# One quarter of the output weights ahead of two v tiles in the load queue, and the scaling of those tiles later on VectorE

## The chip, the cores and the metric

The kernel runs on one core of a Trainium2 chip. The metric is the time of one execution on the device, in microseconds; lower is better. Each comparison runs both kernels in turn on the same chip. A run counts as fast unless it lies more than 1.5% above the fastest of its kernel; ratios use fast runs alone.

## The reference, cut to what matters

Attention with a learned decay, then a feed-forward network on its result:

```python
scores = q @ k.T / sqrt(64)                       # 8 batches x 8 heads, 576 x 576, causal
bias   = -(cum[i] - cum[j])                       # cum = cumsum(max(s, 0))
attn   = softmax(scores + min(bias, 0))
x      = (attn @ v) -> 4608 tokens x 512
out    = gelu(x @ w_in) @ w_out                   # w_in 512 x 2048, w_out 2048 x 512
```

The kernel uses that the row part of the bias cancels in the softmax: it multiplies row j of v, and a column of ones that gives the denominator, by exp(cum[j]). So every v tile is *scaled* by VectorE before it is used.

## The kernel before

The 4608 tokens are worked in 9 chunks of 512. In chunk c TensorE does layer 1 (`w_in`), then layer 2 (`w_out`), and attention of batch c + 1 is woven into layer 2, item by item, so that TensorE never has to stand. Within chunk 0 the loads have not finished yet. The order of the transfers is that of GpSimd's program:

```python
def load_w(which, i):            # a quarter of w_in or w_out: fp32 in HBM, bf16 in SBUF
    ...
        dst = w_out_r[:, i * 4 : (i + 1) * 4, :]          # 4 of the 16 row tiles
    nc.gpsimd.dma_start(out=dst, in_=src)

# start-up (cut)
load_qks(1)
load_w(1, 0)
load_w(1, 1)
load_v(1, nc.gpsimd, (0, 1))     # v tiles 0 and 1 of batch 1
load_w(1, 2)                     # "quarter 2": row tiles 8 to 11 of w_out
load_w(1, 3)                     # "quarter 3": row tiles 12 to 15
load_v(1, nc.gpsimd, (2, 3, 4))
...
# layer 2 of chunk 0 (cut): side[i] is what stands behind the i-th group of matmuls
side[0] = [(sc, b, 0, 0), (scale_v, b, 0), (scale_v, b, 1), (mk, b, 0, 0)]
side[3] = [(sc, b, 1, 0), (to_xT, 0, 4, True), (mk, b, 1, 0)]
side[5] = [(sc, b, 0, 1), (av, b, 0, 0), (av, b, 0, 1)]
side[6] = [(av, b, 1, 0, True), (av, b, 1, 1, True), (scale_v, b, 2), (mk, b, 0, 1)]
...
groups(c, (0, 1), side[:8])      # group i: row tiles 2i and 2i+1, for two blocks of 128 tokens
```

`sc` is a score unit: matmuls on TensorE, then two exponentials on ScalarE. `mk` applies the causal mask (VectorE), `scale_v` scales a v tile (VectorE), `av` is an attention product (TensorE, then two short steps of VectorE), `to_xT` transposes a finished tile (TensorE, then a VectorE copy). A group is four matmuls. Groups 4 and 5 need quarter 2; groups 6 and 7 need quarter 3.

Of the kernel before, what the change touches and what calls it, by code (L numbers as in the profile page):

```python
# [19 lines left out]
def kernel(  # L20
# [89 lines left out]
    def load_qks(b):  # L110
        load_qk(b, 0)
        load_qk(b, 1)

    def raw_v(b):
        raws[b, "v"] = work.tile([128, ST, H, D], fp32, tag="rawv", bufs=2, name="raw_v")
        return raws[b, "v"]

    def load_v(b, eng, sts=range(ST)):
        t = raws[b, "v"] if (b, "v") in raws else raw_v(b)
        for st in sts:  # L120
            n_st = 128 if st < ST - 1 else SL
            eng.dma_start(  # L122
                out=t[:n_st, st, :, :],
                in_=bass.AP(
                    tensor=v.tensor,
                    offset=v.offset + b * H * S * D + st * 128 * D,
                    ap=[[D, n_st], [S * D, H], [1, D]],
                ),
            )
# [11 lines left out]
    def load_w(which, i):  # L141
        if which == 0:
            src = moe_w_in.rearrange("(ko p) f -> p ko f", p=128)[:, :, i * 512 : (i + 1) * 512]
            dst = w_in_r[:, :, i * 512 : (i + 1) * 512]
        else:
            src = moe_w_out.rearrange("(fo p) m -> p fo m", p=128)[:, i * 4 : (i + 1) * 4, :]
            dst = w_out_r[:, i * 4 : (i + 1) * 4, :]
        nc.gpsimd.dma_start(out=dst, in_=src)
# [64 lines left out]
    def square_v(b, st):  # L213
        n_st = 128 if st < ST - 1 else SL
        sq = work.tile([128, H * D], bf16, tag="sq", bufs=2, name="sq")
        nc.scalar.activation(  # L216
            sq[:n_st], raws[b, "v"][:n_st, st].rearrange("p h d -> p (h d)"), func=AF.Square,
            accum_out=sumv[:n_st, b, st : st + 1],
        )
# [11 lines left out]
    def den_col(b):  # L231
        nc.vector.tensor_copy(vv[b % 2][:, :, :, D], wb[:, :, b * H : (b + 1) * H])
# [228 lines left out]
    def l1_item(c, f2, n0=0, n1=NB):  # L461
        if f2 == 0 and n0 == 0:
            gT_of[c] = work.tile([128, FT, NB], bf16, tag="gT", bufs=1, name="gT")
        if n1 - n0 < NB and f2 % 4 < 2:
            h_ps = yps.tile([128, 2, NB // 2], fp32, tag="mlp", bufs=2, name="h2_ps")
        else:
            h_ps = ps.tile([128, 2, NB], fp32, tag="sc", bufs=2, name="h_ps")
        h_ps = h_ps[:, :, : n1 - n0]
        for i in range(2):
            ft = f2 * 2 + i  # L470
            for ko in range(KO):
                nc.tensor.matmul(  # L472
                    h_ps[:, i, :], lhsT=w_in_r[:, ko, ft * 128 : (ft + 1) * 128],
                    rhs=xT[:, ko, c * NB + n0 : c * NB + n1],
                    start=(ko == 0), stop=(ko == KO - 1),
                )
        nc.scalar.activation(  # L477
            gT_of[c][:, f2 * 2 : f2 * 2 + 2, n0:n1], h_ps, func=AF.Gelu
        )
# [24 lines left out]
    def exp_set():  # L504
        nc.scalar.preload_act_table_set("natural_log_exp_and_others")  # L505
# [29 lines left out]
    load_qks(1)  # L535
    load_w(1, 0)
    load_w(1, 1)
    load_v(1, nc.gpsimd, (0, 1))
    load_w(1, 2)
    load_w(1, 3)  # L540
    load_v(1, nc.gpsimd, (2, 3, 4))
    tr_qk(0, 0, 0)
# [30 lines left out]
    sc, mk, av = sc_item, mk_item, av_item  # L573
# [5 lines left out]
    for c in range(NCH):  # L579
        b = c + 1  # L580
        if c > 0 and b + 1 < B:
            load_qks(b + 1)
            load_v(b + 1, nc.gpsimd)
        if c == 0:

            late = [
                [], [], [], [], [(av, 0, 0, 2), (av, 0, 1, 2)],
                [(av, 0, 0, 3), (av, 0, 1, 3)], [(to_xT, 0, 2, True), (to_xT, 0, 3, True)],
                [], [(scale_v, 0, 4), (av, 0, 0, 4)], [(av, 0, 1, 4)],
            ] + [[]] * 6  # L590
            for half in range(2):
                for f2 in range(FT // 2):
                    l1_item(0, f2, half * 256, half * 256 + 256)
                    for f, *a in late[8 * half + f2]:
                        f(*a)
                    if f2 % 2 and 3 <= 8 * half + f2 <= 11:
                        square_v(0, 4 * half + f2 // 2 - 1)
        else:
            for f2 in range(FT // 2):
                l1_item(c, f2)  # L600
                for g, it in late_of.get(c, [])[f2 : f2 + 1]:
                    av(c, g, it)
                if b < B and f2 < HG:
                    tr_qk(b, 0, f2)
                    tr_qk(b, 1, f2)
                if b < B and f2 == 2:
                    den_col(b)
                    for st in range(2):
                        scale_v(b, st)
                if b < B and f2 == 3:  # L610
                    for st in range(2, ST):
                        scale_v(b, st)
                if b < B and 4 <= f2 < 4 + HG:
                    absmax(b, f2 - 4)
                if c == 2 and f2 == 7:
                    cert_decay()
                if f2 < ST and c < B:
                    square_v(c, f2)
        if b < B:
            if c == 0:  # L620
                for g in range(HG):
                    for i in range(2):
                        tr_qk(b, i, g)
                den_col(b)
            exp_set()
            if c == 0:
                load_qks(2)
                load_v(2, nc.gpsimd)
                side = [[] for _ in range(16)]
                side[0] = [(sc, b, 0, 0), (scale_v, b, 0), (scale_v, b, 1), (mk, b, 0, 0)]  # L630
                side[3] = [(sc, b, 1, 0), (to_xT, 0, 4, True), (mk, b, 1, 0)]
                side[5] = [(sc, b, 0, 1), (av, b, 0, 0), (av, b, 0, 1)]
                side[6] = [(av, b, 1, 0, True), (av, b, 1, 1, True), (scale_v, b, 2), (mk, b, 0, 1)]
                side[7] = [(to_xT, b, 0, True), (sc, b, 1, 1)]
                side[8] = [(to_xT, b, 1, True), (scale_v, b, 3), (av, b, 0, 2), (gelu_set,), (mk, b, 1, 1)]
                side[9] = [(av, b, 0, 3)]
                side[11] = [(av, b, 1, 2, True), (scale_v, b, 4), (square_qk, 0, 0, 0), (square_qk, 0, 0, 1)]
                side[12] = [(av, b, 1, 3, True), (square_qk, 0, 1, 0), (square_qk, 0, 1, 1)]
                side[13] = [(to_xT, b, 2, True)]
                side[14] = [(to_xT, b, 3, True)]  # L640
                groups(c, (0, 1), side[:8])
                for sub in (2, 3):
                    groups(c, (sub,), side[4 * sub : 4 * sub + 4])
            else:

                side = [[] for _ in range(16)]
                sc_at = (1, 4, 6, 8) if b < 4 else (1, 4, 7, 10)
                for at, (g, u) in zip(sc_at, [(0, 0), (1, 0), (0, 1), (1, 1)]):
                    side[at].append((sc, b, g, u))
                side[sc_at[3]].append((gelu_set,))  # L650
                mk_at = (4, 6, 8, 10) if b < 4 else (4, 7, 10, 13)
                for at, (g, u) in zip(mk_at, [(0, 0), (1, 0), (0, 1), (1, 1)]):
                    side[at].append((mk, b, g, u))
                for at, (g, it) in zip((5, 6, 8, 9), [(0, 0), (0, 1), (1, 0), (1, 1)]):
                    side[at].append((av, b, g, it))
                if b < 4:
                    side[10].append((av, b, 0, 2))
                    side[11].append((av, b, 1, 2))

                    side[15].extend([(av, b, 0, 3), (av, b, 1, 3)])  # L660
                if c == 1:
                    side[0].append((absmax, c, 0))
                    side[12].extend([(square_qk, c, 1, 0), (square_qk, c, 1, 1)])
                    side[3].append((cert_exp,))
                for sub in range(4):
                    groups(c, (sub,), side[4 * sub : 4 * sub + 4])
        else:
            for sub in range(4):
                l2_item(c, (sub,), store=(c, sub) < LAST)
                if c == B - 1:  # L670
                    (cert_1, cert_2, cert_3, cert_4)[sub]()
                elif sub == 0:

                    rv = nc.values_load(bad[0:1, 0:1], min_val=0, max_val=1)
# [169 lines left out]
```

## Time and profile before

| | before |
|---|---|
| median of 3 runs | 313.47 us (312.7 to 313.74) |
| span of the profile | 311.6 us |
| TensorE busy | 304.0 us, 98% |
| VectorE, ScalarE busy | 196.5, 193.3 us |
| TensorE's waits after the first 8 us | one, 0.52 us, for a quarter of w_out |

"Busy" is the time in which an engine has an instruction under way, "span" the time from its first to its last. How to read the table: TensorE is the bound nearly everywhere, so an instruction of another engine, or a transfer, costs time only where TensorE has to stand for it. The lines that carry this are in the prediction.

How to read the lines of the profile: start in us, length in us, engine (PE is TensorE, DVE VectorE, ACT ScalarE, POOL GpSimd), line of the kernel, operation, what it writes `<-` what it reads, shapes, number of instructions (x8), and in brackets how long the engine stood idle before it and what ended that. Idle times under 0.15 us are not noted, and they count from the modelled end of the instruction before, so a delay can be somewhat larger than its bracket. x7 or x3 where the program has 8 or 4 matmuls means that a record is missing from the trace. The tiles: `o_ps` is layer 2's output and `av` an attention product, both in PSUM, the memory that TensorE writes its results to; `sc_ps` are scores, `P` their exponentials, `xt_ps` transposes.

### The profile page before, as it was taken

What the parts mean: (1) busy time and instruction counts of PE and PEld (TensorE: products, weight loads), DVE (VectorE), ACT (ScalarE), POOL (GpSimd) and SP (SyncE); (2) the same over time, 40 slices, a digit from 0 to 9 for tenths busy, and PEclk for the clock granted to TensorE, in tenths of its full rate; (3) what the DMA queues carried; (4) which work ended last, traced back from release to release, by engine and by line L of the source; (5) the groups of instructions that cost most, each with busy time, mean ns of one, the idle gap of its engine ahead of it and who ended that gap; (6) DMA issues with size and microseconds to landing.
All of it is one profiled execution on the core that took longest, in us unless ns stands there. A gap on an engine that the chain in (4) does not pass through costs nothing. (4 is left out here: it accounts for less than half of the span.)

```text
span 311.6 us, 6102 instructions
## 1 busy us (share of the span) xinstructions
PE 304.0 (98%) x2511; PEld 155.1 (50%) x2511; DVE 196.5 (63%) x397; ACT 193.3 (62%) x262; POOL 53.2 (17%) x72
## 2 busy tenths in 40 slices
PE   6999999999999999999999999999999999999994
PEld 2579655444554455445454545444544555444441
DVE  6976667697769775966498549955895632250010
ACT  2787868878858772974687548765776667105500
POOL 8373340142002400060007000500000000000000
PEclk9999999999999999999999999999999999999999
DMA  7999999769640974089208941633101311010012
GB/s 150 213 231 209 225 216 284 153 139 202 159 99 17 213 171 119 8 177 212 86 18 175 219 95 30 144 69 103 50 19 42 103 53 25 34 68 36 0 69 76
DMA packets 33027, 36.73 MB, mean 118 GB/s; under 512 B 17760, under 2 KB 22112, under 8 KB 32992
## 3 DMA queue, kind: packets, MB, share of 16 engines
q0 software_dynamic: 11472, 22.81, 37.3%
q1 hardware_dynamic: 20336, 12.93, 14.9%
q10 hardware_dynamic: 1184, 0.52, 0.6%
q8 instruction: 21, 0.34, 0.4%
q14 instruction: 14, 0.11, 0.1%
HBM read 36.85 MB, written 9.44 MB: 149 GB/s over the span
## 5 line engine op out<-in xcount | busy, mean ns | idle before, releaser
L488 PE MATMUL o_ps<-w_out_r,gT 128*128 128x512 bf16 x576 | 135.6, 379 | 0.5 <-DMA w_out_r<-in_moe_w_out_dram 0.5
L472 PE MATMUL h_ps<-xT,w_in_r 128*128 128x512 bf16 (+1 forms) x640 | 131.6, 358 | 0.0
L477 ACT ACTIVATE gT<-h_ps 128x1024 bf16<-128x1024 f32 (+1 forms) x80 | 75.1, 938 | 65.7 <-PE h_ps L472 64.7
L472 PEld LDWEIGHTS <-w_in_r 128*128 128x128 bf16 x640 | 60.0, 98 | 54.3 <-issue 0.3
L488 PEld LDWEIGHTS <-gT 128*128 128x128 bf16 x576 | 52.0, 98 | 57.4 <-issue 3.3
L364 ACT ACTIVATE P<-sc_ps 128x1024 bf16<-128x1024 f32 x56 | 54.3, 1021 | 25.8 <-PE sc_ps L349 25.8
L500 DVE COPY o_sb<-o_ps 128x512 f32<-128x512 f32 x30 | 20.7, 691 | 55.7 <-PE o_ps L488 55.7
L122 POOL DMA_DIRECT2D raw_v<-in_v_dram x39 | 33.1, 858 | 126.3 <-ACT sq L216 115.2
L188 DVE STREAM_TRANSPOSE qkT<-raw_qk 128x576 f32<-128x576 f32 x32 | 37.2, 1238 | 0.0
L450 DVE TENSOR_TENSOR x<-av,rc 128x256 bf16<-128x256 f32 (+1 forms) x80 | 33.8, 423 | 3.0
L449 DVE RECIPROCAL rc<-av 128x4 f32<-128x4 f32 (+1 forms) x80 | 14.1, 176 | 34.2 <-PE av L440 34.1
L440 PEld LDWEIGHTS <-P 128*128 128x128 bf16 x576 | 26.5, 98 | 15.8 <-DVE P L372 1.6
L208 DVE TENSOR_REDUCE amx<-raw_qk 128x2 f32<-128x2304 bf16 x13 | 32.7, 2535 | 0.0
L440 PE MATMUL av<-vv,P 128*128 128x65 bf16 x576 | 30.2, 193 | 0.1
L224 DVE TENSOR_TENSOR vv<-raw_v,wb 128x512 bf16<-128x512 f32 (+1 forms) x39 | 25.3, 691 | 3.6 <-DMA raw_v<-in_v_dram 3.6
L216 ACT ACTIVATE sq<-raw_v 128x512 bf16<-128x512 f32 (+1 forms) x40 | 24.8, 621 | 0.0
L372 DVE TENSOR_TENSOR P<-P,tri_bf 128x1024 bf16<-128x1024 bf16 (+1 forms) x33 | 22.7, 692 | 3.3 <-ACT P L364 3.2
L349 PE MATMUL sc_ps<-qkT 32*128 32x256 bf16 (+2 forms) x560 | 18.0, 250 | 0.0
L349 PEld LDWEIGHTS <-qkT 32*128 32x128 bf16 x560 | 11.7, 92 | 12.2 <-issue 8.5
L505 ACT ACT_TABLE_LOAD x8 | 10.3, 1283 | 1.3 <-PEq L828 1.2
L424 PE MATMUL f_ps<-zero 128*128 128x512 bf16 x30 | 9.8, 451 | 1.2 <-DVE zero L151 1.2
L508 ACT ACT_TABLE_LOAD x8 | 10.3, 1283 | 0.1
(80 smaller groups left out, 92.6 us busy)
## 6 DMA issues: line engine op xcount, KB each, us to landing
out_dram<-o_sb SPq DMA_DIRECT2D x34, 256.0 KB, 2.2
raw_v<-in_v_dram POOLq DMA_DIRECT2D x31, 256.0 KB, 5.8
raw_qk<-in_q_dram POOLq DMA_DIRECT2D x7, 576.0 KB, 7.8
raw_qk<-in_k_dram POOLq DMA_DIRECT2D x7, 576.0 KB, 10.7
w_in_r<-in_moe_w_in_dram POOLq DMA_DIRECT2D x4, 512.0 KB, 10.5
w_out_r<-in_moe_w_out_dram POOLq DMA_DIRECT2D x4, 512.0 KB, 15.9
raw_v<-in_v_dram POOLq DMA_DIRECT2D x8, 128.0 KB, 6.0
raw_qk<-in_q_dram POOLq DMA_DIRECT2D x2, 288.0 KB, 6.2
```

Of the source, the lines that this page charges most:

```text
L122: eng.dma_start(out=t[:n_st, st, :, :], in_=bass.AP(tensor=v.tensor, offset=v.offset + b * H * S * D + st * 128 * D, ap=[[D, n_st], [S * D ...
L188: nc.vector.transpose(qkT[b % 2][:, i, g, :S, :].rearrange("p s e -> p (s e)").bitcast(fp32) .rearrange("p (l j) -> p j l", j=LT), raws[b, ...
L208: nc.vector.tensor_reduce(amx[:, b * HG + g], raws[b, "qk"][:, :, g, :], axis=AX, op=ALU.max, apply_absolute_value=True,)
L216: nc.scalar.activation(sq[:n_st], raws[b, "v"][:n_st, st].rearrange("p h d -> p (h d)"), func=AF.Square, accum_out=sumv[:n_st, b, st : st ...
L224: eng.tensor_tensor(vv[b % 2][:n_st, st, :, 0:D], raws[b, "v"][:n_st, st, :, :], w.unsqueeze(2).to_broadcast([n_st, H, D]), op=MULT,)
L349: nc.tensor.matmul(s_ps[h // 2][:, h % 2, off : off + n], lhsT=qk[r, 1, g, jt * 128 : jt * 128 + 128, e], rhs=qk[r, 0, g, i0 : i0 + n, e], ...
L364: nc.scalar.activation(P[:, 2 * h2 : 2 * h2 + 2, o : o + 512], s_ps[h2], func=AF.Exp, scale=scale)
L440: nc.tensor.matmul(o_ps[:, h, :], lhsT=P[:, h, off : off + 128], rhs=vv[b % 2][:, jt, 4 * g + h, :], start=(i == 0), stop=(i == len(BLK[it ...
L450: nc.vector.tensor_tensor(x_of[b, it][:n, g * 256 : g * 256 + 256].rearrange("p (h d) -> p h d", d=D), o_ps[:n, :, 0:D], rc[:n].unsqueeze( ...
L472: nc.tensor.matmul(h_ps[:, i, :], lhsT=w_in_r[:, ko, ft * 128 : (ft + 1) * 128], rhs=xT[:, ko, c * NB + n0 : c * NB + n1], start=(ko == 0) ...
L477: nc.scalar.activation(gT_of[c][:, f2 * 2 : f2 * 2 + 2, n0:n1], h_ps, func=AF.Gelu)
L488: nc.tensor.matmul(y_of[c, sub], lhsT=gT[:, ft, sub * 128 : (sub + 1) * 128], rhs=w_out_r[:, ft, :], start=(ft == 0), stop=(ft == FT - 1),)
```

## The change

The intent: bring quarter 2 of w_out earlier, since TensorE stands for it, and let VectorE wait for the two v tiles only after it has done the mask and the copy that need no v.

```diff
     load_w(1, 1)
+    load_w(1, 2)
     load_v(1, nc.gpsimd, (0, 1))
-    load_w(1, 2)
     load_w(1, 3)
@@
-                side[0] = [(sc, b, 0, 0), (scale_v, b, 0), (scale_v, b, 1), (mk, b, 0, 0)]
-                side[3] = [(sc, b, 1, 0), (to_xT, 0, 4, True), (mk, b, 1, 0)]
+                side[0] = [(sc, b, 0, 0), (mk, b, 0, 0)]
+                side[3] = [
+                    (sc, b, 1, 0), (to_xT, 0, 4, True), (scale_v, b, 0), (scale_v, b, 1), (mk, b, 1, 0)
+                ]
```

## The prediction

> **What bounds the kernel now.** I read the busy shares first, then all that TensorE ever waited for, then the order of time around the one wait that the change can touch.
>
> ```profile
> PE 304.0 (98%) x2511; PEld 155.1 (50%) x2511; DVE 196.5 (63%) x397; ACT 193.3 (62%) x262; POOL 53.2 (17%) x72
> ```
>
> TensorE is busy 304.0 of the 311.6 us span, and the granted clock is full in every slice of the page. VectorE and ScalarE stand at 63% and 62%. So an instruction of VectorE, ScalarE or the transfer queue costs time only where TensorE is made to stand still. The list of TensorE's waits says where it did (engine, line, cause: us, times, longest):
>
> ```profile
> PE t_ps L247 <- ACT cum L241: 1.6, 1, 1.6
> PE f_ps L424 <- DVE zero L151: 1.2, 1, 1.2
> PE o_ps L488 <- DMA w_out_r<-in_moe_w_out_dram: 0.5, 1, 0.5
> ```
>
> These are all. The first two lie in the first 8 us, before the stage the change touches. The third is the whole target: 0.52 us, once, on the third quarter of w_out. TensorE's order of time shows it (start, length, operation, then the idle time before it):
>
> ```profile
> 39.34 0.63 PE L349 MATMUL sc_ps<-qkT 32*128 32x256 bf16 x16
> 39.91 0.29 PE L415 MATMUL xt_ps<-ident_bf,x 64*128 64x64 bf16 x4
> 40.71 1.89 PE L488 MATMUL o_ps<-w_out_r,gT 128*128 128x512 bf16 x8 [0.52 <-DMA w_out_r<-in_moe_w_out_dram]
> 42.53 0.64 PE L349 MATMUL sc_ps<-qkT 32*128 32x256 bf16 x24
> ```
>
> This is layer 2 of chunk 0. After the second score unit (39.34) and four small transposes (39.91, modelled end 40.19), the eight matmuls on w_out rows of the third quarter can't start before 40.71. VectorE in the same stretch:
>
> ```profile
> 37.52 0.70 DVE L224 TENSOR_TENSOR vv<-raw_v,wb 128x512 bf16<-128x512 f32 x1 [2.23 <-DMA raw_v<-in_v_dram]
> 38.51 0.69 DVE L224 TENSOR_TENSOR vv<-raw_v,wb 128x512 bf16<-128x512 f32 x1 [0.29 <-DMA raw_v<-in_v_dram]
> 39.20 0.69 DVE L372 TENSOR_TENSOR P<-P,tri_bf 128x1024 bf16<-128x1024 bf16 x1
> 40.23 0.29 DVE L418 COPY xT<-xt_ps 128x256 bf16<-128x256 bf16 x1 [0.34 <-PE xt_ps L415]
> 41.98 0.69 DVE L372 TENSOR_TENSOR P<-P,tri_bf 128x1024 bf16<-128x1024 bf16 x1 [1.46 <-ACT P L364]
> 43.44 0.18 DVE L449 RECIPROCAL rc<-av 128x4 f32<-128x4 f32 x1 [0.76 <-PE av L440]
> ...
> 45.78 0.68 DVE L224 TENSOR_TENSOR vv<-raw_v,wb 128x512 bf16<-128x512 f32 x1
> ```
>
> It scales v tiles 0 and 1 of batch 1 as they land (37.52, 38.51), masks the first P tile (39.20), copies a transposed tile to xT (40.23), masks the second P tile (41.98), and at 43.44 takes up the first attention output. ScalarE's exponentials, which feed the masks:
>
> ```profile
> 37.23 1.94 ACT L364 ACTIVATE P<-sc_ps 128x1024 bf16<-128x1024 f32 x2
> 40.01 1.94 ACT L364 ACTIVATE P<-sc_ps 128x1024 bf16<-128x1024 f32 x2 [0.84 <-PE sc_ps L349]
> ```
>
> GpSimd's issues of the transfers that the change reorders (w_out quarter 1; v tiles 0 and 1; w_out quarters 2 and 3):
>
> ```profile
> 20.14 0.75 POOL L148 DMA_DIRECT2D w_out_r<-in_moe_w_out_dram  x1 [0.99 <-DMA w_in_r<-in_moe_w_in_dram]
> 21.71 1.86 POOL L122 DMA_DIRECT2D raw_v<-in_v_dram  x2 [0.82 <-DMA raw_v<-in_v_dram]
> 25.33 1.51 POOL L148 DMA_DIRECT2D w_out_r<-in_moe_w_out_dram  x2 [1.76 <-DMA w_in_r<-in_moe_w_in_dram]
> ```
>
> Looking at one issue at a time, the time to landing counts from the start of the issue: w_out quarter 1 16.3 us, v tiles 15.8 each, quarter 2 15.3, quarter 3 17.4. So the landings are: quarter 1 at 20.14 + 16.3 = 36.44; v0 at 21.71 + 15.8 = 37.5; v1, issued about 22.65, at 38.45; quarter 2 at 25.33 + 15.3 = 40.63; quarter 3 at about 26.1 + 17.4 = 43.5. The consumers agree: VectorE starts at 37.52 and 38.51, TensorE at 40.71. A v tile takes about 1.0 us of this queue and quarter 2 takes 40.63 - 38.45 = 2.18 us.
>
> **What the Trainium skill says.** "DMA: Bandwidth & Descriptors", section "Two DMAs through the same engine are not ordered": descriptors of one queue on one DMA engine start in order, but are pipelined, so only the completion semaphore tells that data has landed. The trace agrees as far as it shows: issued in the order quarter 1, v0, v1, quarter 2, they land in that order 1.06, 0.95 and 2.18 us apart. This is what lets me treat the swap as an exchange of places in a line.
> "TensorE: Matmul & The Clock Gate", section "Wait — 56ns, not 53.3ns?": a warm matmul of 512 columns starts 215.7 ns after the one before. The trace's layer 2 run of 16 matmuls from 84.08 to 87.54 gives 3.46/16 = 0.216 us, so the cadence is already the floor, and the 379 ns mean in the table of groups is overlapped length. Same page, section "What's actually happening": the clock falls after an idle window of about 3.4 us. The wait of 0.52 us is far shorter and the clock record stays full, so removing it brings no second gain through the clock.
> The same page, section "Architectural detail: the array is 16× 32×32, not 1× 128×128", says that VectorE's queue is strictly first in, first out. So a scaling that waits for v holds up every later instruction of VectorE. The trace fits: at 38.51 VectorE waits for v1, while P's exponentials end at 37.23 + 1.94 = 39.17, and nothing of later order runs before. That is why the change has to move the scalings too.
>
> **The change part by part.** It adds and removes no instruction; the compiled order of VectorE and GpSimd differs at these places, and TensorE, ScalarE and the store queue keep theirs.
>
> 1. Transfers. Quarter 2 goes ahead of v0 and v1. It lands at 36.44 + 2.18 = 38.62 instead of 40.63. v0 lands at 38.62 + 1.06 = 39.7 (2.2 later), v1 at 40.65 (2.2 later). After the three the line is as before, so quarter 3 (43.5), v2 (27.98 + 17.2 = 45.2) and the rest should land as before.
>
> 2. TensorE. It reaches the third quarter at 40.19 at the latest; the data has then been there for 1.5 us. The 0.52 us go. Its weights were loaded at 40.12 and the transposes are tiny, so it may be up to 0.1 us more.
>
> 3. VectorE. Now mask (0,0) follows the column copy, and runs at about 39.2 (end of the exponentials, 39.17) to 39.85, as before. The xT copy stays at 40.23 to 40.5. Scaling v0: landed 39.7, so 40.5 to 41.2. Scaling v1: landed 40.65, so 41.2 to 41.8. Two scalings of 0.69 us thus go into the hole of 1.46 us before 41.98 that waits for ScalarE's exponentials (40.01 + 1.94 = 41.95). Mask (1,0) still starts at 41.98. So VectorE gains and loses nothing: the waits at 37.5 and 38.5 vanish and the 1.46 us hole is filled.
>
> 4. Who needs those results next. The first attention product stood at 43.10 and comes at about 42.58; it needs v0 scaled (41.2) and the second product v1 scaled (41.8). Slack: 1.4 and 1.0 us. The products on the second P tile come at 43.8 and need mask (1,0), done at 42.65.
>
> Sum: TensorE gets 0.52 us, less at most 0.1 us of new small waits (below), plus at most 0.1. I take 0.5 us. There is no other TensorE wait in the remaining 270 us that could swallow it, and the chain at the end is layer 2, two half copies and a store, so it should reach the end whole. 313.47 - 0.5 = 312.97. The other two runs of before (312.7, 313.74) give a mean of 313.30, so the median may stand a little high; I say 312.9.
>
> **Rivals.** (a) *The score tiles become the wait.* Score unit (0,1) moves from 42.53 to 42.01. It writes two PSUM tiles, and the second comes free only when ScalarE's second exponential ends at 41.95. The margin shrinks from 0.58 to 0.06 us, about the time of a handover (mask (1,0) started 0.03 after). This can take back 0 to 0.1 us, which is in the sum. It would give 313.0 to 313.1.
> (b) *v arrives late.* If small v packets suffer from neighbours and v1 lands after 42.1, then VectorE's queue holds mask (1,0) and the second attention product. v1 would have to be 1.4 us later than I work out for the product to feel it. Against it: 0.95 to 1.06 us each for v0 and v1 in the same stretch. Result if true: gain falls to 0 to 0.3 us, 313.2 to 313.5.
> (c) *The next transfer becomes the wait.* Quarter 3 lands at 43.5; TensorE wants it at 44.94 now and at 44.4 after: 0.9 us of slack. v2 lands at 45.2; VectorE's scaling stood at 45.78 with no wait and would now come at about 45.26: hardly a wait, and only on VectorE. Each issue of GpSimd also waits for the landing of the transfer eight places before it (33.83, 36.44, 37.5 landing; issues at 34.10, 36.75, 37.78), so the k load of batch 2, which waited for v0, now waits for quarter 2 and is issued about 1.1 us later. Some 15 us of transfers stand in line then, and k landed at 37.78 + 15.4 = 53.2 while its first transpose ran at 58.10. It can't matter.
> (d) *Nothing at all.* The wait is hidden anyway, or the gain drowns: runs of before spread over 1.04 us, twice the gain. The first half I hold for unlikely, as TensorE is the bound on both sides of the wait; the second is likely for a single pair of runs.
>
> **Range and chances.** The step is 0.3 to 0.65 us with confidence; the spread of a median of a few runs is about 0.3 us and so is the uncertainty of the 313.47. Together 312.3 to 313.6. Two per cent is 6.3 us, twelve times all that is at stake, and no wait in the stretch could grow so far: v landing several us late would be needed. I give 0.985 to within 2%.
>
> **What would show it.** In the changed kernel: TensorE's list of waits has lost the line on w_out, or keeps under 0.1 us; the eight matmuls after the small transposes start near 40.15; the score unit (0,1) near 42.0, and ScalarE's next pair of exponentials at about 42.7 instead of 43.21; VectorE shows mask, copy, scaling, scaling, mask with the second mask still at 41.98 to 42.0; quarter 2 lands near 38.6, v0 near 39.7, v1 near 40.7; the span is 311.1. I am wrong if quarter 2 still lands after 40.2, if VectorE waits for v past 42, or if TensorE stands as long at another place, such as the scores at 42 or quarter 3.

## The result, and the profile after

| | before | after |
|---|---|---|
| median of 5 runs | 313.47 us (312.7 to 314.35) | 312.9 us (312.3 to 313.32) |
| ratio of fast runs | | 0.998 (95%: 0.9956 to 1.0004) |
| span of the profile | 311.6 us | 311.5 us |

The ratio is the mean time of the one kernel's fast runs over that of the other's in the same rounds, so not quite the ratio of the medians. The median fell on the predicted 312.9. But the interval of the ratio contains 1, and the profiled span did not fall by 0.5 us as it should have; it fell by 0.1. (That profile was taken of the slowest of the five runs, 313.32 us.) So the profiles have to say what happened.

TensorE's waits in the profile after, all of them (engine, line, cause: us, times, longest), are two, both in the first 9 us:

```profile
PE t_ps L247 <- ACT cum L241: 2.1, 1, 2.1
PE f_ps L424 <- DVE zero L151: 1.2, 1, 1.2
```

The line on w_out is gone, as predicted. TensorE's order of time in layer 2 of chunk 0 (no idle time is noted):

```profile
40.41 0.29 PE L415 MATMUL xt_ps<-ident_bf,x 64*128 64x64 bf16 x4
40.63 1.90 PE L488 MATMUL o_ps<-w_out_r,gT 128*128 128x512 bf16 x8
42.46 0.67 PE L349 MATMUL sc_ps<-qkT 32*128 32x256 bf16 x24
43.06 0.54 PE L440 MATMUL av<-vv,P 128*128 128x65 bf16 x12
43.44 1.03 PE L488 MATMUL o_ps<-w_out_r,gT 128*128 128x512 bf16 x4
44.30 0.76 PE L440 MATMUL av<-vv,P 128*128 128x65 bf16 x12
44.90 1.02 PE L488 MATMUL o_ps<-w_out_r,gT 128*128 128x512 bf16 x4
```

VectorE's, with mask, copy, two scalings and mask in the predicted order:

```profile
39.70 0.69 DVE L372 TENSOR_TENSOR P<-P,tri_bf 128x1024 bf16<-128x1024 bf16 x1 [3.91 <-ACT P L364]
40.73 0.29 DVE L418 COPY xT<-xt_ps 128x256 bf16<-128x256 bf16 x1 [0.34 <-PE xt_ps L415]
40.94 1.29 DVE L224 TENSOR_TENSOR vv<-raw_v,wb 128x512 bf16<-128x512 f32 x2
42.48 0.69 DVE L372 TENSOR_TENSOR P<-P,tri_bf 128x1024 bf16<-128x1024 bf16 x1 [0.25 <-ACT P L364]
```

All steps of the prediction seem to be there. But the eight matmuls on quarter 2 start at 40.63, not at 40.15: everything is 0.5 us late, and that comes from the start of the kernel. The first VectorE step on s, before and then after:

```profile
5.15 0.45 DVE L239 TENSOR_SCALAR s_pos<-s_sw 64x576 f32<-64x576 f32 x1 [1.15 <-DMA s_sw<-in_s_dram]
```

```profile
5.41 0.70 DVE L239 TENSOR_SCALAR s_pos<-s_sw 64x576 f32<-64x576 f32 x1 [1.40 <-DMA s_sw<-in_s_dram]
```

It started 0.26 us later, because s landed later, and took 0.25 us more. TensorE's transposes of the summed s hang on it (7.95 us before, 8.45 after), and so layer 1 of chunk 0 began at 19.13 us in the profile before and at 19.63 us in the profile after. No line of the change touches this: it is scatter of the executions. To leave it out I measure from here on from the start of layer 1 to the start of the last copy of the result (two half copies, which the view shows as one line): 307.47 - 19.13 = **288.34 us before, 307.43 - 19.63 = 287.80 us after.** By this measure the predicted 0.5 us are there in full.

That is still no proof. The transfers do not hang on layer 1. If TensorE comes 0.5 us later to the same landing times, the wait of 0.52 us would have vanished with no change at all. This is the question for the experiments.

### The profile page after: what moved, and what is told of

Same layout as the page of the kernel before. It is cut to its first block, busy times and chain, and to the rows that moved or that the text cites. A ratio compares the mean times of both kernels' runs of the same rounds, so it can differ in the third digit from the quotient of the medians.

```text
span 311.5 us, 6102 instructions
## 1 busy us (share of the span) xinstructions
PE 303.9 (98%) x2511; PEld 155.1 (50%) x2511; DVE 195.2 (63%) x397; ACT 193.3 (62%) x262; POOL 53.1 (17%) x72
## 5 line engine op out<-in xcount | busy, mean ns | idle before, releaser
L372 DVE TENSOR_TENSOR P<-P,tri_bf 128x1024 bf16<-128x1024 bf16 (+1 forms) x33 | 22.0, 670 | 6.6 <-ACT P L364 5.9
```

## The experiments

Twelve kernels ran, in three jobs of four. All gave correct results. In the table of all profiles, quarter 2 is "wanted" 21.0 us and quarter 3 23.8 us after the start of layer 1; both are read off the kernels that had no wait (after: 40.63 - 19.63 = 21.00 and 43.44 - 19.63 = 23.81; e7 below: 42.88 - 19.07 = 23.81). Landings are the start of the issue plus its time to landing, good to 0.1 us. "Layer 1 to end" is the measure of above.

| kernel | layer 1 starts | quarter 2 landed / wanted | quarter 3 landed / wanted | layer 1 to end |
|---|---|---|---|---|
| before | 19.13 | 40.63 / 40.1 | 43.5 / 42.9 | 288.34 |
| e10, before again | 19.14 | 40.78 / 40.1 | 43.5 / 42.9 | 288.44 |
| e3, only the scalings moved | 19.25 | 39.90 / 40.2 | 42.85 / 43.1 | 287.82 |
| after | 19.63 | 38.88 / 40.6 | 43.41 / 43.4 | 287.80 |
| e1, after again | 18.97 | 38.82 / 40.0 | 43.35 / 42.8 | 288.15 |
| e11, after again | 19.29 | 39.03 / 40.3 | 43.48 / 43.1 | 288.03 |
| e12, after again | 18.90 | 38.41 / 39.9 | 42.86 / 42.7 | 287.81 |
| e2, only the transfers moved | 19.04 | 38.33 / 40.0 | 42.73 / 42.8 | 287.80 |
| e4, quarter 3 ahead as well | 19.17 | 38.43 / 40.2 | 42.00 / 43.0 | 290.60 |
| e5, before, one more transfer | 19.06 | 41.65 / 40.1 | 43.98 / 42.9 | 289.40 |
| e6, after, one more transfer | 19.10 | 39.07 / 40.1 | 43.42 / 42.9 | 288.10 |
| e7, after, quarter 3 in halves | 19.07 | 38.23 / 40.1 | 42.08 and 42.95 / 42.9 | 287.80 |
| e8, as e7, one more transfer | 18.89 | 38.30 / 39.9 | 41.36 and 42.77 / 42.7 | 287.81 |
| e9, before, both in halves | 19.17 | 39.01 and 40.3 / 40.2 | 41.50 and 42.88 / 43.0 | 287.82 |

(For a quarter in halves, the wanted time is that of the first half; the second is wanted about 0.9 us later for quarter 2, and 1.5 us later for quarter 3.) Seven of the profiles lie at 287.80 to 287.82 us, and none lower. I call this the floor; what is above it is a wait.

### First job: is the gain real, and which half of the change makes it?

**e1_again.** The changed kernel, unaltered.

> The changed kernel unaltered, run again. Theory A (the wait on w_out's third quarter was the whole gain): ratio to before 0.997 to 0.9995 again, the mean about 0.5 us lower, and TensorE's waits have no line on w_out. From the start of layer 1 of chunk 0 to the last copy of the end, which leaves the start-up out, before took 307.47 - 19.13 = 288.34 us; theory A says 287.8 here (the changed kernel's profile: 307.43 - 19.63 = 287.80). Rival B (the wait vanished in the profile after only because TensorE came 0.5 us later from the start-up, and nothing is gained): ratio 1.000 with a mean within 0.15 us of before.

Measured: 313.2 us median against 313.61 for before, ratio 0.999 (0.9973 to 1.0007). (One of the eleven runs of before in this job took 633.89 us and is not among the fast runs.) 288.15 us from layer 1 to the last copy, not 287.8. Layer 1 started early this time, at 18.97 us, and TensorE's list of waits and its order of time show a line that theory A did not have:

```profile
PE o_ps L488 <- DMA w_out_r<-in_moe_w_out_dram: 0.4, 1, 0.4
```

```profile
43.35 1.02 PE L488 MATMUL o_ps<-w_out_r,gT 128*128 128x512 bf16 x4 [0.40 <-DMA w_out_r<-in_moe_w_out_dram]
44.21 0.53 PE L440 MATMUL av<-vv,P 128*128 128x65 bf16 x12
44.58 1.02 PE L488 MATMUL o_ps<-w_out_r,gT 128*128 128x512 bf16 x4
```

Rival B falls as far as quarter 2 goes: it landed at 38.82, 1.2 us before even this early TensorE wanted it. But a wait is back, on the next quarter: until 43.35 TensorE stands for quarter 3. Set beside it the lines of the kernel *before*; the first is for these same four matmuls, which the prediction had passed over:

```profile
43.48 1.03 PE L488 MATMUL o_ps<-w_out_r,gT 128*128 128x512 bf16 x4
44.34 0.76 PE L440 MATMUL av<-vv,P 128*128 128x65 bf16 x12
44.94 1.03 PE L488 MATMUL o_ps<-w_out_r,gT 128*128 128x512 bf16 x4
```

Before took up quarter 3 at 43.48, after having lost 0.58 us (40.71 against 40.13 wanted) to quarter 2; and quarter 3 landed at 26.1 + 17.4 = 43.5. It came just in time because TensorE was late already. Take the first wait away and the second takes its place.

**e2_transfers_only.** The first hunk of the diff alone.

```diff
     load_w(1, 1)
+    load_w(1, 2)
     load_v(1, nc.gpsimd, (0, 1))
-    load_w(1, 2)
     load_w(1, 3)
```

> Quarter 2 ahead of v0 and v1, but VectorE's scalings stay ahead of the first mask. By the slack that I worked out: v1 lands near 41.0, scaled by 41.7, first mask done by 42.4, xT copy 42.6, second mask 43.3; TensorE wants them at 42.6, 42.9 and 43.8. So theory A says the wait is gone and nothing, or at most 0.3 us, comes in its place: as fast as the changed kernel (0.998, 287.8 to 288.1 us from layer 1 to the last copy). Rival C (the scalings had to move, as I wrote in the prediction): TensorE stands 0.5 us or more at the first attention products or behind the transposes' PSUM tile, ratio 1.000 or above.

Measured: 313.7 us median, ratio 1.0001 (0.998 to 1.0022), six runs from 312.59 to 314.02; 287.80 us from layer 1 to the last copy, and no wait of TensorE on w_out, on v or on a PSUM tile. VectorE:

```profile
39.51 0.69 DVE L224 TENSOR_TENSOR vv<-raw_v,wb 128x512 bf16<-128x512 f32 x1 [4.31 <-DMA raw_v<-in_v_dram]
40.49 0.70 DVE L224 TENSOR_TENSOR vv<-raw_v,wb 128x512 bf16<-128x512 f32 x1 [0.28 <-DMA raw_v<-in_v_dram]
41.10 0.69 DVE L372 TENSOR_TENSOR P<-P,tri_bf 128x1024 bf16<-128x1024 bf16 x1
41.70 0.29 DVE L418 COPY xT<-xt_ps 128x256 bf16<-128x256 bf16 x1
41.90 0.68 DVE L372 TENSOR_TENSOR P<-P,tri_bf 128x1024 bf16<-128x1024 bf16 x1
```

The mask (39.0 in e1) comes at 41.10, the copy at 41.70 and the second mask at 41.90, all in time, for TensorE's first attention product has no idle time before it:

```profile
42.47 0.54 PE L440 MATMUL av<-vv,P 128*128 128x65 bf16 x12
```

So in this execution the scalings need not have moved; theory A's slack was right here, and rival C, which stood in my own prediction ("the change has to move the scalings too"), falls for it. The times of this kernel do not show the gain of the trace: the profiled run is the second fastest of six that scatter over 1.4 us, and their mean, 313.51 us, is that of before (313.56), while e1 has 313.21. Six runs do not tell 313.51 from 313.21, so whether scalings left in their place cost something in other executions stays open.

**e3_scalings_only.** The second hunk alone.

```diff
-                side[0] = [(sc, b, 0, 0), (scale_v, b, 0), (scale_v, b, 1), (mk, b, 0, 0)]
-                side[3] = [(sc, b, 1, 0), (to_xT, 0, 4, True), (mk, b, 1, 0)]
+                side[0] = [(sc, b, 0, 0), (mk, b, 0, 0)]
+                side[3] = [
+                    (sc, b, 1, 0), (to_xT, 0, 4, True), (scale_v, b, 0), (scale_v, b, 1), (mk, b, 1, 0)
+                ]
```

> The scalings moved behind the second score unit, transfers in the order of before. Theory A: the wait on the third quarter stays, about 0.5 us less what TensorE's start-up was late; 288.2 to 288.4 us from layer 1 to the last copy with a start like before's, ratio 1.000. Rival C (VectorE's order is what pays): wait or not, ratio 0.998 and 287.8 us.

Measured: 313.52 us median, ratio 0.9995 (0.9977 to 1.0013). The trace surprised both theories: no wait at all, 287.82 us.

```profile
40.25 1.90 PE L488 MATMUL o_ps<-w_out_r,gT 128*128 128x512 bf16 x8
```

The transfers stand in the order of before, yet quarter 2 landed at 39.90, 0.7 us earlier than in the profile of before, and TensorE took it up at 40.25 with nothing to wait for. VectorE can't have done that: its scalings come after the landing. It is scatter of the load queue (the quarter ahead of it, untouched by anything, landed at 35.7 here, at 36.4 in before). So the wait of 0.52 us that the whole change aims at is one draw: it exists in some executions and not in others. E10 below is another draw of before.

**e4_both_quarters.** Quarter 3 goes ahead of v too.

```diff
     load_w(1, 2)
+    load_w(1, 3)
     load_v(1, nc.gpsimd, (0, 1))
-    load_w(1, 3)
```

> The changed kernel with quarter 3 ahead of v0 and v1 too. Quarter 3 took 2.2 to 2.9 us of the queue, so v0 lands near 42.5 and v1 near 43.5, scaled by 43.2 and 44.2. Theory A with my slack of 1.0 to 1.4 us for v: TensorE stands 0.5 to 1.2 us at the first two attention products, 288.3 to 289.0 us from layer 1 to the last copy, ratio 1.000 to 1.002. If v has much more slack than that: 287.8 us and 0.998.

Measured: 315.93 us median, ratio 1.0078 (1.0052 to 1.0103); 290.60 us, 2.8 above the floor. TensorE:

```profile
43.90 0.32 PE L440 MATMUL av<-vv,P 128*128 128x65 bf16 x5 [1.24 <-DVE vv L224]
45.28 0.37 PE L440 MATMUL av<-vv,P 128*128 128x65 bf16 x7 [1.06 <-DVE vv L224]
```

It stands 1.24 and 1.06 us for the scaled v tiles (and 0.25 us more soon after). I had the right place and at most half the size: quarter 3 landed 42.00 - 38.43 = 3.6 us after quarter 2, against the 2.2 to 2.9 that I reckoned with, so v1 landed at 44.5 and not at 43.5. So v can't be moved back by another quarter, and the way out for quarter 3 is not to overtake v as a whole.

### Second job: where does the wait go?

The new theory, D, is that TensorE has two appointments with the same queue, 2.8 us apart, and that whoever brings the first forward meets the second. Waits of half a microsecond drown in the scatter, so I made them larger: one more v tile is read, into a tile that nothing uses, behind quarter 1.

```diff
     load_w(1, 1)
+    extra = work.tile([128, H, D], fp32, tag="extra", bufs=1, name="extra")
+    nc.gpsimd.dma_start(out=extra, in_=...)      # 128 x 8 x 64 of v, as load_v reads it
```

**e5_before_late.** Before, with that edit.

> The kernel before, with one more v tile read into a tile that nothing uses, right behind w_out's second quarter: it takes 1.0 to 1.1 us of the queue, so quarters 2 and 3 and v0, v1 land that much later, which makes the disputed waits large against their scatter from run to run. New theory D, from the profiles so far: quarter 3 lands 2.85 us after quarter 2 in before, and TensorE needs it 2.77 us after it has taken up quarter 2, so both quarters wait for the same queue, and what moves quarter 2 forward leaves the wait to quarter 3. D and old A agree on this kernel: TensorE stands 1.0 to 1.6 us at quarter 2, 288.8 to 289.4 us from layer 1 to the last copy (287.8 with no wait), ratio 1.002 to 1.004.

Measured: 314.35 us median, ratio 1.0037 (1.0024 to 1.0049); 289.40 us.

```profile
41.71 1.89 PE L488 MATMUL o_ps<-w_out_r,gT 128*128 128x512 bf16 x7 [1.58 <-DMA w_out_r<-in_moe_w_out_dram]
```

As both theories say: 1.58 us of wait at quarter 2, and the time rises with it, 1.1 us by the trace (289.40 - 288.34) and 1.06 us by the mean of the runs (314.41 - 313.35). A microsecond of TensorE's wait here is a microsecond of the whole kernel; nothing later absorbs it.

**e6_after_late.** The changed kernel with that edit.

> The changed kernel with the same extra transfer. Theory A (the wait on quarter 2 is all there is): no wait, 287.8 to 288.0 us, over 1 us faster than the kernel before with the extra transfer, ratio to before 0.998 to 0.9995. Theory D: no wait at quarter 2, but TensorE stands 0.9 to 1.6 us at quarter 3 (landing near 44.2 to 44.6, wanted at 42.8 to 43.4), 288.7 to 289.4 us, and as slow as the kernel before with the extra transfer to within 0.3 us: ratio 1.002 to 1.004.

Measured: 313.87 us median, ratio 1.0021 (1.0008 to 1.0033); 288.10 us.

```profile
43.44 1.02 PE L488 MATMUL o_ps<-w_out_r,gT 128*128 128x512 bf16 x4 [0.37 <-DMA w_out_r<-in_moe_w_out_dram]
```

Neither theory has it whole. Theory A's "no wait" is refuted: the wait is at quarter 3, where D puts it. But D's size is refuted too: this kernel is faster than e5 by 313.87 - 314.35 = -0.48 us in the medians (0.52 in the means, and of its six runs only the slowest lies among those of e5). The reason is in the table: D took from before that quarter 3 lands 2.85 us after quarter 2, as long as TensorE needs from the one to the other. In e5 it landed 43.98 - 41.65 = 2.33 us after, and in e6 at 43.42. What there is to gain is the lag of quarter 2 less the lag of quarter 3, each against the moment at which an unhindered TensorE wants it; in e5's own execution 1.6 us against 43.98 - 42.87 = 1.1 us (of which some 0.2 us costs nothing, as will be seen). D had set the two equal.

**e7_split.** The changed kernel, quarter 3 as two transfers of two row tiles each.

```diff
-    load_w(1, 3)
+    for f0 in (12, 14):
+        nc.gpsimd.dma_start(
+            out=w_out_r[:, f0 : f0 + 2, :],
+            in_=moe_w_out.rearrange("(fo p) m -> p fo m", p=128)[:, f0 : f0 + 2, :],
+        )
```

> The changed kernel with quarter 3 of w_out as two transfers of half its rows, in the same place, so its first half should land about 1.2 us before the second. Theory D: TensorE needs the first half at 42.8 to 43.4 (lands near 42.2) and the second 1.2 us later; no wait on w_out at all whatever the start-up, 287.8 us from layer 1 to the last copy, ratio 0.998 to 0.9995. Theory A: the same as the changed kernel, waits of 0 to 0.4 us only by chance. In the time alone the two are hard to tell apart; the next kernel decides.

Measured: 313.0 us median, ratio 0.9994 (0.9979 to 1.001); 287.80 us, no wait on w_out. The first half landed at 42.08, 0.87 us before the second; I had said 1.2.

**e8_split_late.** The same with the extra transfer.

> Split quarter 3 and the extra transfer. Theory D: first half lands near 42.9 to 43.5, TensorE stands 0 to 0.4 us there and at most 0.2 at the second half; v1 lands near 42.0, so 0 to 0.2 us at the attention product: 287.9 to 288.4 us, ratio 0.999 to 1.001, some 1 us faster than the changed kernel with the extra transfer. If it stands as long as that kernel, 1 us or more, the landing of quarter 3 is not what held it, and D falls.

Measured: 313.28 us median, ratio 1.0002 (0.9989 to 1.0016); 287.81 us. These four matmuls on the first half of quarter 3:

```profile
42.70 1.03 PE L488 MATMUL o_ps<-w_out_r,gT 128*128 128x512 bf16 x4
```

No idle time, and by the means of six runs each e8 is 313.89 - 313.33 = 0.56 us faster than e6. Their programs differ in one thing: in e8 quarter 3 comes in halves, so that TensorE needs at first only the first. So far this supports D.

A caution belongs here. The profiled execution of e8 had an early queue: quarter 1 landed at 35.0, against 35.7 in e6, and even the *second* half of quarter 3 landed at 42.77, when a whole quarter would have been wanted at 42.7. The same holds for e7 (42.95 against 42.9). In these two executions the whole quarter would have cost nothing either, because 0.2 us of wait at this place are given back, as will be seen. That TensorE is held by quarter 3 is shown by e1 and e6, whose matmuls start within 0.1 us of its landing; that halving it helps rests on the times of e8 against e6, not on the trace of e8; and whether the early queue was chance stays open.

### Third job: finer pieces without reordering, and more draws

**e9_split_only.** Before, with both quarters in halves and nothing else.

```diff
-    load_w(1, 2)
-    load_w(1, 3)
+    for f0 in (8, 10, 12, 14):
+        nc.gpsimd.dma_start(
+            out=w_out_r[:, f0 : f0 + 2, :],
+            in_=moe_w_out.rearrange("(fo p) m -> p fo m", p=128)[:, f0 : f0 + 2, :],
+        )
```

> The order of the kernel before, v0 and v1 first, scalings where they were; but quarters 2 and 3 of w_out each as two transfers of half their rows. Theory D (each piece of w_out has its own moment, and the wait is for whole quarters of which only half is wanted): first half of quarter 2 lands near 39.6 (wanted 21.0 us after the start of layer 1, about 40.1), its second half near 40.6 (wanted about 41.0), first half of quarter 3 near 42.1 (wanted 23.8 us after, about 42.9), second near 43.4 (wanted about 44.3): no wait on w_out of over 0.1 us, 287.8 to 287.9 us from layer 1 to the last copy, as fast as the changed kernel or up to 0.4 us faster, with no reordering. If the order is what matters: a wait of 0.3 us or more stays at quarter 2.

Measured: 312.92 us median, ratio 0.9997 (0.9966 to 1.0027, wide because one of its six runs took 315.32 us); 287.82 us, no wait on w_out.

```profile
40.16 1.90 PE L488 MATMUL o_ps<-w_out_r,gT 128*128 128x512 bf16 x7
...
42.98 1.03 PE L488 MATMUL o_ps<-w_out_r,gT 128*128 128x512 bf16 x4
```

The halves landed at 39.01, 40.3, 41.50 and 42.88, each before it was wanted. Its queue was a middling one, quarter 1 landing at 36.0 against 36.4 in before and 35.7 in e3. Without the split, by my estimate, quarter 2 would have been there as a whole at the 40.3 of its second half, about 0.1 us late for 40.2, so this profile shows 1.3 us of added room and hardly a wait that was saved. In the times it is not shown to be faster than the changed kernel.

**e10_before_again.**

> The kernel before, once more, for its waits in another execution and its mean. Theory D: a wait of 0 to 0.6 us at quarter 2, none of weight at quarter 3; which it is follows from quarter 2's landing less 21.0 us after the start of layer 1. Mean 313.3 to 313.6 us.

Measured: 313.7 us median, ratio to the other runs of the same kernel 1.0007 (0.9987 to 1.0026); 288.44 us, 0.61 us of wait at quarter 2:

```profile
40.81 1.89 PE L488 MATMUL o_ps<-w_out_r,gT 128*128 128x512 bf16 x7 [0.61 <-DMA w_out_r<-in_moe_w_out_dram]
```

The ratio of a kernel to itself misses 1 by 0.0007, or by 0.3 us in the means (313.74 against 313.44). So a difference of 0.3 us in such a comparison is nothing to build on.

**e11_after_again.**

> The changed kernel, once more. Theory D: no wait at quarter 2, 0 to 0.5 us at quarter 3, equal to its landing less 23.8 us after the start of layer 1; mean 0.1 to 0.5 us below the kernel before of the same chip. Theory A: none at either, 0.5 us below.

Measured: 313.23 us median, ratio 0.9989 (0.9969 to 1.0009); 288.03 us. The matmuls on quarter 3 start at 43.55 instead of 43.10, held by its landing at 43.48.

**e12_after_third.**

> The changed kernel, a third time, for the same numbers: D has 0 to 0.5 us at quarter 3 and a mean 0.1 to 0.5 us below before; A has no wait and 0.5 us.

Measured: 312.91 us median, ratio 0.9985 (0.9966 to 1.0004); 287.81 us. Quarter 3 held TensorE for 0.2 us, and the 0.2 us came back at once, for a reason given below.

## Why the prediction was right or wrong

**The number was right, the reason only in part.** 312.9 was predicted and measured. The mechanism behind it was right in its first half and wrong in its second; that one median met the number to the digit, with a scatter of 1 us, is luck.

**Right: the queue is a line in which places can be exchanged.** Quarter 2 was to land near 38.6; it landed at 38.9, 38.8, 39.0 and 38.4 in four profiles of the changed kernel. v0 and v1 were to land at 39.7 and 40.65; they landed at 40.0 and 41.0 in the profile after. TensorE never waited for quarter 2 again. What did not carry over is the length of each step: quarter 2 landed 2.18 us after v1 in the profile before, but 38.9 - 36.3 = 2.6 us after quarter 1 in the profile after, which is why v0 and v1 came 0.3 us later than predicted.

**Right: VectorE has room.** Both scalings went into the hole before the second mask, which started at its usual place relative to TensorE. But the sentence that the scalings *had* to move fell with e2: left where they were, they delay the first mask by 2.1 us and the copy by 1.6 us against e1, and the second mask by 0.1 us, and all three had that much room. Nor did the line that the prediction gave for VectorE's strict order show it: at 38.51 the mask could not have run anyway, since its exponentials end at 39.17. E2 shows it: there the exponentials end at 37.14 + 1.94 = 39.08, and the mask still stands behind the two scalings until 41.10.

**Right: rival (a) costs next to nothing.** With the wait gone, the score unit takes 43.06 - 42.46 = 0.60 us to the next product instead of 43.10 - 42.53 = 0.57. That is 0.03 us; up to 0.1 was allowed.

**Wrong: rival (c), the next transfer.** The step that failed reads: "Quarter 3 lands at 43.5; TensorE wants it at 44.94 now and at 44.4 after: 0.9 us of slack." I had taken the matmuls at 44.94 for the first on quarter 3. They are the second group on it. The first is at 43.48, two lines above in the same view of the trace (both lines are shown under e1; the prediction's excerpt ends before them). With the wait removed TensorE wants quarter 3 at 42.9, so the slack was not +0.9 but -0.6 us. Had I counted the groups in the program (group 6 is the first of quarter 3, and stands behind the two `av` of `side[5]`), I would have found it. By the numbers of before alone the sum should then have read as follows:

- Wait removed: 40.71 - 40.13 = 0.58 us, of which 0.54 count (288.34 - 287.80).
- Wait that takes its place: 43.5 - 42.94 = 0.55 us at quarter 3.
- Of this, 0.23 us costs nothing. Without a wait, the next two attention products are themselves held up until VectorE frees a PSUM tile: 44.90 - 44.30 = 0.60 us in the profile after, where VectorE's step on the product before runs until 44.16 + 0.42 = 44.58 and eight of the twelve matmuls start after it. Behind a wait at quarter 3 VectorE has caught up (that step ends at 43.51 + 0.42 = 43.93 in e1, before the products start): 44.58 - 44.21 = 0.37 us. The same sum fits e1 (wait 0.57, less 0.23 makes 0.34; measured 0.35), e6 (0.53, 0.30; 0.30), e11 (0.45, 0.22; 0.23) and e12 (0.21, none; 0.01).
- Gain: 0.54 - 0.32 = about 0.2 us in that execution, not 0.5.

The two steps of VectorE, in the profile after and then in e1:

```profile
44.16 0.42 DVE L450 TENSOR_TENSOR x<-av,rc 128x256 bf16<-128x256 f32 x1
```

```profile
43.51 0.42 DVE L450 TENSOR_TENSOR x<-av,rc 128x256 bf16<-128x256 f32 x1
```

This line of reasoning is worked out and not run for that one execution; but its two parts are shown, by e1 and e6 for the wait on quarter 3, and by e5 for the full weight of the wait on quarter 2.

**Missed: the wait is a draw.** I took 0.52 us from one profile for a property of the kernel. In three profiles with the transfer order of before (before, e10, e3) the loss above the floor was 0.54, 0.64 and 0.02 us, mean 0.40. In five with the order of after (after, e1, e2, e11, e12) it was 0.00, 0.35, 0.00, 0.23 and 0.01, mean 0.12. Two moments decide it, and both shift from one execution to the next, not in step: the start of layer 1 (18.90 to 19.63 us within the one changed kernel) and the landings (quarter 1 at 35.7 to 36.5 us in the same four profiles).

**What the change is worth.** The profiles say 0.40 - 0.12 = about 0.3 us, from few draws. The four comparisons of times gave 0.998, 0.999, 0.9989 and 0.9985 (the last two share the runs of before): all below 1, and each interval reaching past it. 0.3 us is 0.001 of the time. A gain is not proven by any one comparison. Put together, the record does show one: the differences of the means in the three sessions that ran both kernels unaltered (e10 counted with before, e11 and e12 with after) are 0.63, 0.34 and 0.46 us, and over all 32 fast runs of before and 23 of after this makes 0.46 us, with a 95% interval of 0.22 to 0.70 worked out from the scatter within the sessions. The 0.3 us of the few profiles and the predicted 0.5 us both lie in it; which of them is nearer stays open.

**A better version?** E7 and e9 show no wait on w_out in their profiles, and with a burdened queue halves were 0.56 us faster than whole quarters. In the times without the burden e7 (mean 313.06 against 313.35 of before, 0.9994) and e9 are not told apart from the changed kernel. I would still prefer halves to the reordering, for the room they leave; this is a judgement, not a measured gain.

## What to carry to other kernels

When a wait on a transfer is to be removed, list *all* later appointments of the same engine with the same queue, and compute each one's slack with the wait already gone; a landing that looks just in time may only be so because the engine was late. A wait shorter than the scatter of the start and of the queue must be read from several profiles, from a starting point behind the start-up, and it helps to burden the queue on purpose until the wait stands clear of the scatter. And where only half of a transfer is wanted at first, two transfers of half the size bring the first half forward (by 0.9 to 1.4 us against the second here), and the v tile behind them came no later: at 44.5 us in e7, at 44.3 to 45.0 in the four profiles of the changed kernel.

## What the Trainium skill lacked or had wrong

- "DMA: Bandwidth & Descriptors", section "Measured (HBM→SBUF, 128 partitions, SWDGE, issued from GpSimd)", gives the time and efficiency of single transfers by size, with the rule to batch to 1 MiB or more. With other transfers queued ahead and behind, halving a quarter (1 MiB of fp32 in HBM) cost nothing that these runs show: quarter 2 in halves took 40.3 - 38.1 = 2.2 us from v1's landing (e9), and whole 40.63 - 38.44 = 2.19 us (before) and 39.90 - 37.69 = 2.21 us (e3).
- No page has how far the landings of transfers and the start-up scatter from one execution to the next, so that a wait in one profile may be one draw ("TensorE: Matmul & The Clock Gate" has it only for the clock's warm-up). Here quarter 2 landed at 39.90, 40.63 and 40.78 us with one transfer order, and layer 1 of one kernel began between 18.90 and 19.63 us.
